# Second network: other places in memory for the activation tiles, and one load ahead of another

## The chip, the cores and the metric

The kernel runs on one core of one Trainium2 chip. The metric is the device time of one launch in microseconds (us). The engines are TensorE (PE, with its weight loads as PEld), VectorE (DVE), ScalarE (ACT), GpSimd (POOL) and SyncE (SP); SP issues nearly all transfers between HBM and the on-chip memory in this part of the program.

## The reference

The reference chains three stages: a thresholded attention, a layer of eight experts (each token goes to one), and a dense two-layer network. The last one, cut to what matters here:

```python
def _moe2_ref(x, w_in, w_out, alpha) -> np.ndarray:      # x (2304, 512), w_in (512, 2048), w_out (2048, 512)
    h = x @ w_in
    g = np.maximum(h, 0.0) + alpha * np.minimum(h, 0.0)
    return (g @ w_out).astype(np.float32)
```

Here x is the output of the expert layer; its gate weight is multiplied onto the result of the dense network, at the end.

## The kernel before

All matrix products are done in split form: each fp32 operand is cast to a high part and a low part (fp32r), and three products (high by high, high by low, low by high) are summed. So every operand costs a cast on ACT and a subtraction on DVE or POOL before PE can use it.

**The expert layer** (`experts`) runs over 8 experts by 8 chunks of 128 hidden columns, 64 steps of the index g. PE computes `l` (lines 1059 to 1061) and then `y` (1096 to 1098). After the last chunk of an expert its result is copied from PSUM to the tile `yT` (line 1104, ACT and DVE share the work for the last expert) and written to HBM as `yt_d` (line 1114).

**The second network** (`network`) takes its tokens from `yt_d`, in three rounds of 768 tokens, each in two halves of 384. A half is loaded (line 1474) and split into `yh` and `yl` (lines 1481 and 1482). Per round there are 16 chunks of 128 hidden columns times 2 halves, so 32 steps; a step is one hidden block. `f1` computes a block: 12 matmuls into one of two PSUM banks `h` (lines 1552 to 1554), then DVE makes `t` out of it in two instructions (1556 and 1557; the second frees the bank), ACT casts it to `gh` (1559) and POOL subtracts to `gl` (1560). Two steps later `f2mm` multiplies that block with a chunk of `w_out`: 9 matmuls, in threes of which two read `gh` and one reads `gl` (1570 to 1572). So PE's order is f1 of block one, f1 of block two, f1 of block three, f2mm of block one, f1 of block four, f2mm of block two, and so on.

**The weights of the second network** come as 64-bit numbers and are converted chunk by chunk (`conv`): 16 chunks of `w_in` and the first of `w_out` during the expert layer, the other 15 of `w_out` during the first round. A chunk is loaded by `cvload` (line 1423 for `w_out`) into one of two buffers `raw`. ACT takes its absolute value (1436), DVE makes `f` (1438, 1440, 1442), ACT casts it into the weight tile (1447), DVE makes `r` (1449, 1450; the last read of the buffer), and POOL finishes (1452, 1453). The tokens of a half go into the same two `raw` buffers, except those of the very first half, which use the tile `xs` of the expert layer. `y2["limit"]` is the number of chunks that may have been asked for; `cvload` does nothing beyond it.

**What sets the order.** The scheduler is off (`manual_schedule`): each engine runs its instructions as the code is written. The turn of g = 59 issues the load of the first half (`first`), that of g = 60 issues the second (`second`). Semaphore waits are made by the framework, from the tiles: a tile that is laid over the place of an older one waits for everything that still reads or writes the older one.

**Where the tiles lie.** Pools are laid out one behind another, in the order in which they are opened, and those of the second network begin where those of the experts began. In bytes per partition from that start, the experts' tiles are: `stg` 2080 to 18464, `xs` 18464 to 26656, the weight rings `w1` and `w2` 26656 to 59424, the tokens `x` 59424 to 82464, `h` 82464 to 89376, `yT` 89376 to 96288. Over these lie, before: `os` and the second half's `yh`, `yl` 0 to 20480, the `w_out` chunks 1 to 15 20480 to 81920, `gh` 81920 to 88064, `gl` 88064 to 94208, `t` 94208 to 97280.

Of the kernel before, what the change touches and what calls it, by code (L numbers as in the profile page):

```python
# [28 lines left out]
KF2 = FF2 // 128  # L29
# [123 lines left out]
def attn_moe_ffn(ctx: ExitStack, tc, q, k, v, tau, emb, mtau, w1, w2, w_in, w_out, alpha, out):  # L153
# [1244 lines left out]
    def shared(st, general):  # L1398

        y2 = {}  # L1400
# [4 lines left out]
        y2["wo"] = WO  # L1405
        WO[0] = cv_p.tile([128, 2, DM], F32R, tag="wo0", name="wo0", bufs=1)

        y2["limit"] = KF2 + (1 if general else 2)

        def rawtile():  # L1410
            return cv_p.tile([128, 4 * HB], U32, tag="raw", name="raw")
# [59 lines left out]
        def load(q, hf, t):  # L1471
            y2["yg", hf] = t = t.rearrange("p (k n) -> p k n", k=KD)
            n0 = q * NB + hf * HB
            nc.sync.dma_start(t, yt_d[:, :, n0:n0 + HB])
# [12 lines left out]

        def second(p):
            load(0, 1, rawtile().bitcast(F32))

        y2["load"], y2["split"] = load, split
        y2["ahead"] = [first, second] + [lambda p, c=c: [split(0, x) for x in c] for c in ((), (0,), (1, 2, 3))]
# [2 lines left out]
    def network(general, y2):  # L1495
# [3 lines left out]
        def npool(name, **kw):  # L1499
            return f2.enter_context(tc.tile_pool(name=name, reuse_waits="tile", **kw))  # L1500

        os_p = npool("os", bufs=4)
        if general:
            y2["pool", 0] = npool("yT2", bufs=1)
        y2["pool", 1] = npool("yT3", bufs=1)
        wo_p = npool("wo", bufs=1)
        WO = y2["wo"]
        for c in range(1, KF2):
            WO[c] = wo_p.tile([128, 2, DM], F32R, name=f"wo{c}")
        g_p = npool("g", bufs=4)  # L1510
        t_p = npool("tt", bufs=2)
        ps_h = npool("ps_h", bufs=2, space=PSUM)
        ps_o = npool("ps_o", bufs=2 * HT, space=PSUM)
        G = {}
# [121 lines left out]
    with tc.If(far == 0) as near:  # L1636
        with ExitStack() as st:
            y2 = shared(st, False)
            experts(CAPS_NEAR, False, y2)
            network(False, y2)  # L1640
    with near.Else():
        with ExitStack() as st:
            y2 = shared(st, True)
            experts(CAPS_FAR, True, y2)
            network(True, y2)
# [27 lines left out]
```

## Time and profile before

| what | us |
|---|---|
| median of 3 runs (lowest 1065.16, highest 1066.11) | 1065.36 |
| the profiled execution, its own time | 1063.56 |
| its span, first to last instruction | 1061.4 |

The mean granted TensorE clock of that execution was 0.982 of full speed. Busy times: PE 1008.0 us (95% of the span), DVE 708.5 (67%), POOL 529.0 (50%), ACT 507.6 (48%). The expert layer ends and the second network begins at about 640 us. A timeline row reads: start in us, duration in us, engine, line, operation, output<-input, shapes, count; in square brackets the time that the engine was idle before it and what ended that.

### The profile page before, as it was taken

The page shows a single profiled execution, that of the slowest core. Times are in us where ns is not written, and L with a number is a line of the kernel's source. Part 1 is how long each engine was busy: PE and PEld are TensorE (multiplying, and loading weights), DVE is VectorE, ACT ScalarE, POOL GpSimd, SP SyncE. Part 2 cuts the span into 40 slices and gives each one's busy share as a digit, 9 for nine tenths or more (in the row PEclk, how much of TensorE's full clock was granted, in tenths as well). Part 3 has the DMA queues.
Part 4 walks back from the last instruction along what each step waited for, and adds up shares of the span by engine and source line. Part 5 has one row for each costly group of instructions (what it writes and reads, how often), then busy time and mean ns, then how long its engine had stood idle before and what let it go on. Part 6 is the DMA issues. An engine that isn't in the chain of part 4 may idle for free. (4 is left out here: it accounts for less than half of the span.)

```text
span 1061.4 us, 17732 instructions
## 1 busy us (share of the span) xinstructions
PE 1008.0 (95%) x6224; PEld 908.6 (86%) x6224; DVE 708.5 (67%) x1501; ACT 507.6 (48%) x1074; POOL 529.0 (50%) x610
## 2 busy tenths in 40 slices
PE   7999999999999849999999997999999999999995
PEld 6888888878888738999999996999999999999995
DVE  8988888898889747787868887889642222422321
ACT  5777777788777534555546553232231111311112
POOL 6688786888886432222355223756533222332223
PEclk9999999999999979999999998999999999999998
DMA  4265564433321066686988854222220000000001
GB/s 117 66 186 164 155 170 139 120 116 89 80 67 40 1 200 226 191 266 180 242 204 195 246 166 111 80 63 77 80 90 30 1 1 1 31 30 1 1 1 63
DMA packets 100098, 113.67 MB, mean 107 GB/s; under 512 B 22072, under 2 KB 81464, under 8 KB 100000
## 3 DMA queue, kind: packets, MB, share of 16 engines
q1 hardware_dynamic: 96544, 102.99, 34.5%
q0 software_dynamic: 3456, 9.46, 2.4%
q8 instruction: 51, 0.84, 0.3%
q14 instruction: 47, 0.39, 0.1%
HBM read 75.21 MB, written 28.36 MB: 98 GB/s over the span
## 5 line engine op out<-in xcount | busy, mean ns | idle before, releaser
L1560 POOL TENSOR_TENSOR gl<-t,gh 128x384 fp32r<-128x384 f32 x96 | 102.5, 1068 | 246.5 <-ACT gh L1559 246.5
L1556 DVE TENSOR_SCALAR t<-h,alpha_t 128x384 f32<-128x384 f32 x96 | 59.1, 616 | 206.2 <-PE h L1554 200.7
L1559 ACT CAST gh<-t 128x384 fp32r<-128x384 f32 x96 | 49.3, 513 | 271.3 <-DVE t L1557 162.8
L530 DVE TENSOR_REDUCE mx<-s 128x1 f32<-128x576 f32 x144 | 108.1, 754 | 25.5 <-PE s L523 24.1
L546 DVE SCALAR_TENSOR_TENSOR p<-s,mx,e 128x576 f32<-128x576 f32 x144 | 115.9, 810 | 10.8 <-ACT e L539 7.8
L539 ACT ACTIVATE e<-s,mx 128x576 f32<-128x576 f32 x144 | 107.2, 746 | 14.9 <-DVE mx L530 13.6
L1004 DVE TENSOR_TENSOR w<-stg,w 128x512 fp32r<-128x512 f32 x128 | 107.8, 858 | 9.1 <-ACT w L1003 8.5
L1572 PE MATMUL o<-wo,gl 128*128 128x512 f32 x288 | 113.3, 394 | 0.0
L1571 PE MATMUL o<-wo,gh 128*128 128x512 f32 x288 | 113.1, 393 | 0.0
L1570 PE MATMUL o<-wo,gh 128*128 128x512 f32 x288 | 112.3, 390 | 0.0
L559 PE MATMUL t<-ident,p 128*128 128x128 f32 (+1 forms) x720 | 107.6, 277 | 3.6 <-DVE ptl L377 1.1
L559 PEld LDWEIGHTS t<-ident,p 128*128 128x128 f32 (+1 forms) x720 | 80.9, 137 | 7.5 <-ACT pt L586 3.4
L523 PE MATMUL s<-ks,qs 128*128 128x288 f32 x256 | 80.6, 330 | 6.2 <-DVE p L546 5.3
L1003 ACT CAST w<-stg 128x512 fp32r<-128x512 f32 x128 | 76.7, 619 | 15.8 <-DMA stg<-in_moe_w_dram 15.8
L1097 PE MATMUL y<-h,w 128*128 128x256 f32 (+6 forms) x256 | 80.2, 313 | 2.8 <-DVE h L1065 2.8
L1096 PE MATMUL y<-h,w 128*128 128x256 f32 (+6 forms) x256 | 82.3, 321 | 0.0
L1060 PE MATMUL l<-x,w 128*128 128x256 f32 (+6 forms) x256 | 79.8, 312 | 0.3 <-DVE x L1048 0.2
L1059 PE MATMUL l<-x,w 128*128 128x256 f32 (+6 forms) x256 | 79.9, 312 | 0.0
L1098 PE MATMUL y<-h,w 128*128 128x256 f32 (+6 forms) x256 | 79.6, 311 | 0.0
L1061 PE MATMUL l<-x,w 128*128 128x256 f32 (+6 forms) x256 | 79.5, 310 | 0.0
L523 PE MATMUL s<-kx,qs 128*128 128x288 f32 x256 | 72.9, 299 | 0.2
L1554 PE MATMUL h<-yh,wi_b 128*128 128x384 f32 x216 | 73.0, 338 | 0.0
(233 smaller groups left out, 2756.1 us busy)
## 6 DMA issues: line engine op xcount, KB each, us to landing
stg<-in_moe_w_dram SPq DMA_DIRECT2D x64, 512.0 KB, 5.4
kx<-ks SPq DMA_DIRECT2D x60, 144.0 KB, 2.5
xd<-zt SPq DMA_DIRECT2D x8, 1024.0 KB, 7.5
raw<-in_moe_w_in_dram SPq DMA_DIRECT2D x16, 512.0 KB, 3.7
raw<-in_moe_w_out_dram SPq DMA_DIRECT2D x16, 512.0 KB, 3.5
rawk<-in_k_dram SPq DMA_DIRECT2D x16, 256.0 KB, 2.9
rawq<-in_q_dram SPq DMA_DIRECT2D x16, 256.0 KB, 2.9
yd<-zt SPq DMA_DIRECT2D x4, 1024.0 KB, 6.8
```

The costliest lines, as they stand in the source:

```text
L523: nc.tensor.matmul(s[:, hf, 0:288], lt, st[nm, a][:, hf * 288:(hf + 1) * 288], start=(j == 0 and x == 0), stop=(j == n - 1 and x == 1))
L530: nc.vector.tensor_reduce(out=mx[:, 0:1], in_=st["s", t][:, :, 0:288], op=ALU.min, axis=AX.XY)
L539: nc.scalar.activation(e, st["s", t][:, :, 0:288], AF.Exp, bias=st["mx", t][:, 0:1], scale=-1.0)
L546: nc.vector.scalar_tensor_tensor(out=p.rearrange("q (a b) -> q a b", a=2), in0=st["s", t][:, :, 0:288], scalar=st["mx", t][:, 2:3], in1=st ...
L559: nc.tensor.transpose(m[0:w, j * n + i * 128:j * n + (i + 1) * 128], st["p", t][:, c * 128:c * 128 + w], ident)
L1004: nc.vector.tensor_tensor(t[:, 1], src, t[:, 0].bitcast(F32), op=ALU.subtract)
L1096: nc.tensor.matmul(m[:, 0:n], w[:, 0, dsl], h[:, 0, 0:n], start=(f == 0), stop=False)
L1097: nc.tensor.matmul(m[:, 0:n], w[:, 0, dsl], h[:, 1, 0:n], start=False, stop=False)
L1560: nc.gpsimd.tensor_tensor(gl, g, gh.bitcast(F32), op=ALU.subtract)
L1570: nc.tensor.matmul(m, gh[:, ts], WO[f][:, 0, :], start=(f == 0), stop=False)
L1571: nc.tensor.matmul(m, gh[:, ts], WO[f][:, 1, :], start=False, stop=False)
L1572: nc.tensor.matmul(m, gl[:, ts], WO[f][:, 0, :], start=False, stop=(f == KF2 - 1))
```

## The change

Two edits. The pools of `gh`/`gl` and of `t` are opened ahead of the pool of the `w_out` chunks. And the limit on chunks is one lower until `second` has taken its buffer; `second` then raises it by one. On the path that these inputs take, `general` is false.

```diff
-        y2["limit"] = KF2 + (1 if general else 2)
+        y2["limit"] = KF2 + 1
...
         def second(p):
             load(0, 1, rawtile().bitcast(F32))
+            y2["limit"] += 1
...
         y2["pool", 1] = npool("yT3", bufs=1)
+        g_p = npool("g", bufs=4)
+        t_p = npool("tt", bufs=2)
         wo_p = npool("wo", bufs=1)
         WO = y2["wo"]
         for c in range(1, KF2):
             WO[c] = wo_p.tile([128, 2, DM], F32R, name=f"wo{c}")
-        g_p = npool("g", bufs=4)
-        t_p = npool("tt", bufs=2)
```

With it the second network's tiles lie, from the same start: `gh` 20480 to 26624, `gl` 26624 to 32768, `t` 32768 to 35840, the `w_out` chunks 1 to 15 35840 to 97280, of which chunk 14 is at 89088 to 93184 and chunk 15 at 93184 to 97280. From line 1490 on, a line of the changed kernel has a number one higher than its counterpart before (`t` is made at 1557 and 1558, `gh` at 1560, `gl` at 1561).

SP's queue at the end of the expert layer. `xs<-yt_d` and `raw<-yt_d` are the tokens of the first and the second half, `raw<-in_moe_w_out_dram` are chunks of `w_out`, `yt_d<-yT` is the last expert's result; names such as DMAHW7 are the semaphores of single transfers. Before:

```order
L1474 DMA xs<-yt_d 128x4x384 [waits DMAHW5_49,DMAHW4_49,PE_49]
L1486 DMA gs<-pd 128x18x2 [waits DMASW3_49]
L1423 DMA raw<-in_moe_w_out_dram 128x1024 [waits DMAHW7_49,DVE_49,Activation_49]
L1474 DMA raw<-yt_d 128x4x384 [waits DMAHW0_49,DMAHW2_49,DVE_49,Activation_49]
L1114 DMA yt_d<-yT 512x1x288 [waits DMAHW1_49,DMAHW0_49,DMAHW5_49,DVE_49,Activation_49]
L1423 DMA raw<-in_moe_w_out_dram 128x1024 [waits DVE_49]
```

And now:

```order
L1474 DMA xs<-yt_d 128x4x384 [waits DMAHW5_49,DMAHW4_49,PE_49]
L1486 DMA gs<-pd 128x18x2 [waits DMASW3_49]
L1474 DMA raw<-yt_d 128x4x384 [waits DMAHW7_49,DVE_49,Activation_49]
L1423 DMA raw<-in_moe_w_out_dram 128x1024 [waits DMAHW0_49,DMAHW2_49,DVE_49,Activation_49]
L1114 DMA yt_d<-yT 512x1x288 [waits DMAHW5_49,DMAHW1_49,DMAHW7_49,DVE_49,Activation_49]
L1423 DMA raw<-in_moe_w_out_dram 128x1024 [waits DVE_49]
```

The second half's tokens and the second `w_out` chunk have changed places, and with them the two `raw` buffers and their waits: the tokens now wait for the last `w_in` chunk's buffer, the chunk for the first `w_out` chunk's.

DVE at the same place: the last copies of `yT`, the second half's subtractions (`yl<-raw,yh`), then the first hidden block's `t`. Before:

```order
L1104 COPY yT<-y_8654 128x288 [waits DMAHW4_49,PE_49]
L1104 COPY yT<-y_8662 128x288 [waits PE_49]
L1482 TENSOR_TENSOR yl_8978<-raw,yh_8977 128x384 [waits DMAHW0_49,DVE_49,Activation_49]
L1482 TENSOR_TENSOR yl_8978<-raw,yh_8977 128x384 [waits Activation_49] x3
L1556 TENSOR_SCALAR t<-h,alpha_t 128x384 [waits DMAHW1_49,DVE_49,PE_49]
L1557 SCALAR_TENSOR_TENSOR t<-h,t 128x384 [waits DVE_49]
```

And now:

```order
L1104 COPY yT<-y_8654 128x288 [waits DMAHW4_49,PE_49]
L1104 COPY yT<-y_8662 128x288 [waits PE_49]
L1482 TENSOR_TENSOR yl_8978<-raw,yh_8977 128x384 [waits DMAHW7_49,DVE_49,Activation_49]
L1482 TENSOR_TENSOR yl_8978<-raw,yh_8977 128x384 [waits Activation_49] x3
L1557 TENSOR_SCALAR t<-h,alpha_t 128x384 [waits PE_49]
L1558 SCALAR_TENSOR_TENSOR t<-h,t 128x384 [waits DVE_49]
```

The order on DVE is unchanged. The first `t` waited for a transfer (DMAHW1) besides PE and now waits for PE alone.

POOL around the first `gl`, with the end of the first `w_out` chunk ahead of it and the second chunk behind. Before:

```order
L1453 TENSOR_TENSOR wo_5804<-f,r 128x512 [waits DVE_49,Pool_49]
L1560 TENSOR_TENSOR gl<-t,gh 128x384 [waits DMAHW3_49,DMAHW2_49,DMAHW4_49,DMAHW1_49,DMAHW5_49,DMAHW0_49,DMAHW6_49,PE_49,Activation_49]
L1560 TENSOR_TENSOR gl<-t,gh 128x384 [waits Activation_49]
L1452 TENSOR_TENSOR f<-f,wo_8950 128x512 [waits DVE_49]
L1453 TENSOR_TENSOR wo_8950<-f,r 128x512 [waits DMAHW5_49,DMAHW6_49,DMAHW3_49,DMAHW7_49,DVE_49,Pool_49]
```

And now:

```order
L1453 TENSOR_TENSOR wo_5804<-f,r 128x512 [waits DVE_49,Pool_49]
L1561 TENSOR_TENSOR gl<-t,gh 128x384 [waits DMAHW3_49,DMAHW4_49,DMAHW2_49,DMAHW5_49,DMAHW1_49,DMAHW6_49,DMAHW0_49,DMAHW7_49,PE_49,Activation_49]
L1561 TENSOR_TENSOR gl<-t,gh 128x384 [waits PE_49,Activation_49]
L1452 TENSOR_TENSOR f<-f,wo_8956 128x512 [waits DVE_49]
L1453 TENSOR_TENSOR wo_8956<-f,r 128x512 [waits DVE_49,Pool_49]
```

The order on POOL is unchanged too. The first `gl` waits for transfers in both, the rows do not tell which transfer of each semaphore; the first chunk of `w_out` that is converted in this stage no longer does.

## Rows read from the trace of the kernel before

**Rows 1.** Windows: us, then busy us per engine, granted clock, DMA share, GB/s.

```profile
640.00:656.00 16.00, 9.41 (x44) 8.51 (x44) 8.81 (x18) 4.41 (x10) 1.01 (x1) 0.79 0.48 112
656.00:850.00 194.00, 194.00 (x976) 176.04 (x975) 119.89 (x173) 47.81 (x90) 98.34 (x83) 1.00 0.19 60
850.00:1046.00 196.00, 196.00 (x988) 178.11 (x987) 60.02 (x102) 30.81 (x62) 53.48 (x53) 1.00 0.02 9
```

**Rows 2.** Waits, 630 to 700 us: who waited for whom, total, times, longest.

```profile
PE h L1552 <- DVE t L1557: 5.9, 1, 5.9
DVE t L1556 <- DMA yt_d<-yT: 5.5, 1, 5.5
...
ACT yh L1481 <- DMA raw<-yt_d: 2.0, 1, 2.0
```

**Rows 3.** Timeline of PE.

```profile
642.65 0.34 PE L1554 MATMUL h<-yh,wi 128*128 128x384 f32 x1
...
652.23 0.69 PE L1552 MATMUL h<-yh,wi 128*128 128x384 f32 x1 [5.89 <-DVE t L1557]
...
655.92 0.40 PE L1570 MATMUL o<-wo,gh 128*128 128x512 f32 x1
...
658.03 0.34 PE L1552 MATMUL h<-yh,wi 128*128 128x384 f32 x1
...
660.15 0.39 PE L1570 MATMUL o<-wo,gh 128*128 128x512 f32 x1
```

**Rows 4.** Windows of 2 us within the transition, columns as in rows 1.

```profile
646.00:648.00 2.00, 0.34 (x2) 0.01 (x1) 0.00 (x0) 0.00 (x0) 0.00 (x0) 1.00 0.88 142
...
650.00:652.00 2.00, 0.00 (x0) 0.00 (x0) 1.00 (x2) 0.00 (x0) 0.00 (x0) 0.50 0.21 12
```

**Rows 5.** Timeline of SP.

```profile
631.12 0.63 SPq L1474 DMA_DIRECT2D xs<-yt_d  x1
...
632.53 3.38 SPq L1423 DMA_DIRECT2D raw<-in_moe_w_out_dram  x1
637.27 0.58 SPq L1474 DMA_DIRECT2D raw<-yt_d  x1
643.15 0.63 SPq L1114 DMA_DIRECT2D yt_d<-yT  x1
```

**Rows 6.** Transfers issued from 615 to 690 us: KB each, median us to landing.

```profile
xs<-yt_d SPq DMA_DIRECT2D x1, 768.0 KB, 5.1
...
yt_d<-yT SPq DMA_DIRECT2D x1, 576.0 KB, 7.7
```

**Rows 7.** Line 1423, all 16 loads of `w_out` chunks.

```profile
DMA to landing us min/median/max: 3.4/3.5/6.6
```

**Rows 8.** Timeline of ACT.

```profile
640.55 0.40 ACT L1104 COPY yT<-y 128x288 f32<-128x288 f32 x1 [0.39 <-PE y L1098]
642.97 1.76 ACT L1481 CAST yh<-raw 128x384 fp32r<-128x384 f32 x4 [2.02 <-DMA raw<-yt_d]
644.63 0.67 ACT L1436 ACTIVATE f<-raw 128x512 f32<-128x512 f32 x1
```

**Rows 9.** Timeline of DVE.

```profile
641.18 0.81 DVE L1104 COPY yT<-y 128x288 f32<-128x288 f32 x2
643.52 1.96 DVE L1482 TENSOR_TENSOR yl<-raw,yh 128x384 fp32r<-128x384 f32 x4 [1.53 <-ACT yh L1481]
650.97 0.62 DVE L1556 TENSOR_SCALAR t<-h,alpha_t 128x384 f32<-128x384 f32 x1 [5.49 <-DMA yt_d<-yT]
651.62 0.56 DVE L1557 SCALAR_TENSOR_TENSOR t<-h,t 128x384 f32<-128x384 f32 x1
...
654.97 0.56 DVE L1557 SCALAR_TENSOR_TENSOR t<-h,t 128x384 f32<-128x384 f32 x1
...
657.62 1.39 DVE L1438 TENSOR_SCALAR f<-f 128x512 f32<-128x512 f32 x1
```

**Rows 10.** Timeline of POOL.

```profile
652.86 1.01 POOL L1560 TENSOR_TENSOR gl<-t,gh 128x384 fp32r<-128x384 f32 x1 [12.95 <-ACT gh L1559]
```

## The prediction

> **What bounds the kernel now.** I read the windows first, to see where PE, the busiest engine, is not busy. From 656 to 1046 us it is busy for every one of the 390 us at the full clock, so in that stretch nothing but PE's own work counts, and whatever moves PE's arrival at 656 us moves the end by as much [rows 1]. In the 16 us ahead of it PE is busy for only 9.41 us, at a mean granted clock of 0.79 [rows 1]. That is the hand-over from the expert layer to the second network, and the change touches it.
>
> The waits tell why [rows 2]: PE waits 5.9 us, once, for DVE's `t`, and DVE waits 5.5 us, once, for the transfer `yt_d<-yT`. The reader is to see one chain. The last expert's result is issued at 643.15 [rows 5] and lands 7.7 us later [rows 6]. Only then, at 650.97, does DVE begin the first `t` [rows 9]. It is done at 651.62 + 0.56 = 652.18, which frees the PSUM bank, and PE starts its third hidden block at 652.23 [rows 3]. The numbers in `t` have nothing to do with that transfer. What ties them is the place: `t` lies at bytes 94208 to 97280, over `yT` at 89376 to 96288, which the transfer still reads. While PE stands idle its clock falls from 1.00 to 0.50 of full speed, that is from 2.4 to 1.2 GHz [rows 4], so the third block, 12 matmuls, takes 655.92 - 652.23 = 3.69 us; the fourth takes 660.15 - 658.03 = 2.12 [rows 3].
>
> A smaller wait comes ahead of it. ACT idles 2.0 us for the second half's tokens, `raw<-yt_d`, and starts to split them at 642.97 [rows 2, 8]. They were issued only at 637.27, behind the second `w_out` chunk [rows 5].
>
> **The change part by part.** It adds and removes no instruction; it moves tiles, and exchanges two loads.
>
> *The place of `t`, `gh`, `gl`.* Now `t` and `gl` lie over the ring `w1` and `gh` over `xs`. The last readers are PE's `l` matmuls, ACT's and DVE's splitting of the first half, all over before DVE's copies of `yT` end at 641.18 + 0.81 = 641.99 [rows 9]. So the first `t` waits for PE and for its turn on DVE alone, as DVE's order shows. Over `yT` come the `w_out` chunks 14 and 15, which the code converts in the last turns of the first round, some 28 steps later; the transfer is over by then, and I cost that at nothing. Were it not over, POOL would wait there and PE's `f2mm` of chunk 14 behind it.
>
> *The tokens ahead of the chunk.* They take the place at 632.53 [rows 5]; the buffer is free there, since the chunk could be issued into it. No row shows their landing from this place, so I bound it. Early end: 5.1 us after issue, as the first half's tokens of the same size took [rows 6], 637.6. Late end: the chunk in this place took at most 6.6 us for 512 KB [rows 7], by size 6.6 x 768/512 = 9.9 us, 642.4. I take 640.5, an estimate nearer to the late end, because `xs<-yt_d` is under way until 631.12 + 5.1 = 636.2 and the two share the engines. What decides is whether they are there when ACT has copied its share of `yT`, at 640.55 + 0.40 = 640.95 [rows 8]. With 640.5 they are.
>
> One might fear that the bigger load slows `xs<-yt_d`, which ACT needs at once. In the trace the chunk was issued 1.41 us behind it [rows 5], and it still landed 5.1 us after its own issue [rows 6]. The Trainium skill (DMA: Bandwidth & Descriptors, Queues, rings and completion order) says that transfers of one issuing engine share a row of rings, that a DMA engine takes descriptors in ring order, and that completion is nevertheless not in order. By the first half of the rule the sum stands as below; by the second `xs` could lose time to the 256 KB more behind it, a third of its own size, and the sum would be smaller by about a third of 5.1 us, 1.7.
>
> *The sum*, in the order of the engines.
> ACT starts the second half's casts at 641.0 instead of 642.97. DVE follows as soon as it is free: its four subtractions take 1.96 us [rows 9], 641.99 + 1.96 = 643.95. The two `t` instructions take 652.18 - 650.97 = 1.21 us [rows 9], so the bank is free at 645.16, and with the hand-over of 0.05 (652.23 - 652.18) PE may start the third block at 645.2.
> PE itself: the first block's last matmul starts at 642.65 [rows 3], and 0.17 us later (2.12/12) the second block follows without the gap for tokens, until 642.82 + 2.12 = 644.94. It then waits 0.3 us for the bank, far too short for the clock to fall as it did (it was still at 1.00 in the first 2 us of the idle time [rows 4]). The third block ends at 645.2 + 2.12 = 647.3.
> Then `f2mm` of block one. The first `gl` was ready at 652.86 + 1.01 = 653.87, 1.69 us behind `t` [rows 9, 10]; now 645.16 + 1.69 = 646.85, in time. It starts at 647.3 instead of 655.92 [rows 3]: 8.6 us earlier, of which 652.23 - 645.2 = 7.0 are waiting and 3.69 - 2.12 = 1.6 clock.
>
> Does PE keep it? DVE gains only 652.18 - 645.16 = 7.0, so its lead over PE shrinks by 1.6. The fourth block started at 658.03 [rows 3], its bank had been free since 654.97 + 0.56 = 655.53 [rows 9]: a lead of 2.5 us, now 0.9. It holds. After that the third `w_out` chunk is the late one: its load is issued when the tokens' buffer is free, 643.95, and lands at most 6.6 us later [rows 7], at 650.55; with ACT's 0.67 [rows 8] DVE can begin it at 651.2, while the order would want it at 657.62 - 7.0 = 650.6 [rows 9]. 0.6 us late, inside the lead. The second chunk, issued at 637.27 now, must be there when ACT has cast the tokens, at 641.0 + 1.76 = 642.8; by the 6.6 it lands at 643.9 at the latest, and the first `gh`, behind it on ACT, is due at 645.2 (643.9 + 0.67 = 644.6). Hidden.
>
> Bounds of the sum: if PE never waits it is 655.92 - (644.94 + 2.12) = 8.9. If the tokens land at 642.4, DVE's subtractions begin 0.55 us later (643.52 - 642.97), `t` is done at 642.95 + 1.96 + 1.21 = 646.1, the third block starts at 646.2, and the gain is 7.6.
>
> Span 1061.4 - 8.6 = 1052.8; the profiled execution 1063.56 - 8.6 = 1055.0. The median of the runs was 1.8 above the profiled execution, so 1065.36 - 8.6 = 1056.8 is the time I predict.
>
> **The rivals.**
> *The first `gl` still waits for `yT`.* POOL's row still names transfers, DMAHW1 among them, and that is the semaphore on which `t` waited. If it means the last result, issued at about 642.1 now, `gl` begins at 642.1 + 7.7 = 649.8 and is ready at 650.9, while PE has its third matmul of `f2mm` at 647.8 (nine of them take 658.03 - 655.92 = 2.11, so the third comes 0.5 after the first). PE loses 3.1 us and, as the pause is as long as the one that cost the clock, up to 1.6 more: a gain of about 4.7 to 3.9, 1061.1. Against it: `gl` at 26624 to 32768 shares no byte with `yT`; its first 32 bytes lie over `xs`, which ends at 26656 and was filled by many older transfers, and that explains the list.
> *DVE becomes the bound.* The lead of 0.9 is thin, and DVE's instructions are uneven: 1.39 us for a line that POOL's work beside it stretches [rows 9]. Each such stretch beyond the lead costs about 1.39 - 0.9 = 0.5; with the late third chunk, two to four of them, 1 to 2 us: 1058.3. By the Trainium skill (SBUF — State Buffer, Who interferes with whom) whichever of DVE and GpSimd comes first keeps the shared port for its whole instruction, so a DVE instruction can lose a whole POOL instruction's time; that would make each stretch 1.0 (the 1.01 of rows 10) and this rival 1 to 3 us. For it: the lead. Against it: the stall's end leaves the two engines' relative order as it was.
> *Slower: the second chunk blocks ACT.* It now queues behind 768 KB of tokens, and ACT's absolute value of it stands ahead of the first `gh`. If it lands at T, the first `gl` is ready at T + 0.67 + 1.69, and PE, whose clock would have fallen, pays 1.6 as well. Before, the third matmul of `f2mm` came at 655.92 + 0.5 = 656.4. The change becomes a loss from T = 656.4 - 4.0 = 652.4, 15 us after issue; at T = 656 it would be 3.6 slower, 1069. Against it: no chunk took more than 6.6 [rows 7], and the longest transfer of the place 7.7 [rows 6].
> *The change doesn't do what it says*: another old reader holds the new places, and DVE waits as before, 1065.4. DVE's order, where the transfer is gone from the first `t`, speaks against it.
>
> **How the numbers follow.** My forecast has 0.72, with a range of its own of 1056.0 to 1058.0 (the sum's bounds, and half a us for the spread of the runs). DVE as the bound, or tokens at the late end and more, 0.11; `gl` waiting, 0.06; more than the sum, through a wait that I don't see, 0.04; no effect 0.04; slower 0.03. A measurement of this kernel can tell 0.2%, 2.1 us, from no change, so faster means under 1063.2: 0.72 + 0.11 + 0.06 + 0.04 = 0.93. Same 0.04, slower 0.03. The range from 1055.2 to 1060.2 takes in the forecast, the DVE rival and part of the rest.
>
> **What would show it.** In the profile after: no wait of DVE's first `t` for a transfer, and PE's wait for `t` at the third block under 1 us (if it is still 3 us or more, the place of `t` was not what held it). `raw<-yt_d` issued at about 632.5, ACT casting from about 641 without idling. A granted clock of 1.00 in all windows from 640 to 656 us, and the first `f2mm` at about 647.3. PE busy without a break from there on; new waits of PE for `t` in the first ten blocks would speak for DVE as the bound, a wait for `gl` for the first rival, ACT idle ahead of line 1436 for the slower one. If the span is shorter by less than 7 us, a step of the sum is wrong.

## The result, and the profile after

The changed kernel takes 1057.22 us in the median of 6 runs (1053.46 to 1057.59); the kernel before, run beside it, 1065.28 (1065.06 to 1066.11). The ratio is 0.9917, with a 95% interval from 0.9903 to 0.9931: 0.0083 of 1065.28 is 8.8 us faster, with the interval 7.4 to 10.3; the two medians alone lie 8.1 us apart. Forecast were 8.6 us and 1056.8 us.

The profiled execution of the changed kernel took 1056.95 us, its span 1055.1. Its times can't be laid over those of before directly: it reached the last `y` matmul of the expert layer 2.36 us later, as one row of the kernel before (timeline of PE) shows against the first row of the fence after it.

```profile
640.62 0.29 PE L1098 MATMUL y<-h,w 128*128 128x288 f32 x1
```

The timeline of PE after the change: the last `y` matmul, the first matmuls of the second network's second and third hidden blocks, of the first `f2mm` and of the fourth block. Lines below the edit have moved by one.

```profile
642.98 0.30 PE L1098 MATMUL y<-h,w 128*128 128x288 f32 x1
...
645.20 0.34 PE L1553 MATMUL h<-yh,wi 128*128 128x384 f32 x1
...
647.40 0.45 PE L1553 MATMUL h<-yh,wi 128*128 128x384 f32 x1
...
649.59 0.39 PE L1571 MATMUL o<-wo,gh 128*128 128x512 f32 x1
...
651.69 0.34 PE L1553 MATMUL h<-yh,wi 128*128 128x384 f32 x1
```

So I count from the last `y` matmul. Before, the third block followed 652.23 - 640.62 = 11.61 us later and the first `f2mm` 15.30 [rows 3]; now it is 647.40 - 642.98 = 4.42 and 6.61. `f2mm` is 8.69 us earlier. The third block, from its first matmul to `f2mm`, takes 2.19 where it took 3.69, and the fourth block starts 8.71 after the last `y` matmul where it was 17.41. PE waits no more, and works at the full clock; the windows (columns as in rows 1) answer to [rows 1, 4]:

```profile
640.00:656.00 16.00, 15.62 (x87) 14.30 (x87) 13.71 (x24) 7.30 (x16) 7.66 (x7) 1.00 0.82 183
...
650.00:652.00 2.00, 2.00 (x10) 1.64 (x10) 1.93 (x5) 0.76 (x2) 0.66 (x1) 1.00 1.04 102
...
656.00:850.00 194.00, 194.00 (x979) 176.44 (x978) 120.84 (x171) 47.30 (x88) 95.74 (x82) 1.00 0.18 58
```

The reader is to see 15.62 of 16 us busy at a granted 1.00, for 9.41 at 0.79. The waits of 630 to 700 us answer to [rows 2]; the 5.9 us of PE and the 5.5 of DVE are gone, and the longest wait for a transfer is a new one, of ACT for a `w_out` chunk:

```profile
ACT f L1436 <- DMA raw<-in_moe_w_out_dram: 3.0, 1, 3.0
DVE f L1438 <- ACT f L1436: 2.0, 1, 2.0
...
ACT yh L1481 <- DMA xs<-yt_d: 0.6, 1, 0.6
...
PE y L1097 <- DVE h L1065: 0.4, 1, 0.4
...
ACT yh L1481 <- DMA raw<-yt_d: 0.3, 1, 0.3
```

The timeline of SP shows the exchanged loads, and `yT`'s issue between the second and the third chunk; it answers to [rows 5]:

```profile
633.76 0.63 SPq L1474 DMA_DIRECT2D xs<-yt_d  x1
...
635.18 3.80 SPq L1474 DMA_DIRECT2D raw<-yt_d  x1
639.64 0.36 SPq L1423 DMA_DIRECT2D raw<-in_moe_w_out_dram  x1
644.50 0.63 SPq L1114 DMA_DIRECT2D yt_d<-yT  x1
646.25 5.92 SPq L1423 DMA_DIRECT2D raw<-in_moe_w_out_dram  x2
```

The transfers' rows (KB each, us from issue to landing), one from each of three stretches, answer to [rows 6, 7]; the last is the third chunk:

```profile
xs<-yt_d SPq DMA_DIRECT2D x1, 768.0 KB, 5.6
...
yt_d<-yT SPq DMA_DIRECT2D x1, 576.0 KB, 9.2
...
raw<-in_moe_w_out_dram SPq DMA_DIRECT2D x1, 512.0 KB, 7.9
```

And the timelines of ACT, DVE and POOL, put together in order of time; they answer to [rows 8 to 10]:

```profile
643.61 1.76 ACT L1481 CAST yh<-raw 128x384 fp32r<-128x384 f32 x4 [0.29 <-DMA raw<-yt_d]
...
646.15 0.60 DVE L1557 TENSOR_SCALAR t<-h,alpha_t 128x384 f32<-128x384 f32 x1
...
646.79 0.56 DVE L1558 SCALAR_TENSOR_TENSOR t<-h,t 128x384 f32<-128x384 f32 x1
...
648.03 1.02 POOL L1561 TENSOR_TENSOR gl<-t,gh 128x384 fp32r<-128x384 f32 x1 [5.76 <-ACT gh L1560]
...
650.16 0.56 DVE L1558 SCALAR_TENSOR_TENSOR t<-h,t 128x384 f32<-128x384 f32 x1
...
654.25 0.67 ACT L1436 ACTIVATE f<-raw 128x512 f32<-128x512 f32 x1 [2.98 <-DMA raw<-in_moe_w_out_dram]
...
654.95 0.61 DVE L1438 TENSOR_SCALAR f<-f 128x512 f32<-128x512 f32 x1 [2.05 <-ACT f L1436]
```

`yT` is issued at 644.50 and lands at 653.7, and the first `t` starts at 646.15 without a bracket: it no longer waits for that transfer. `t` is done at 647.35 and PE starts at 647.40.

### The profile page after: what moved, and what is told of

It is laid out like the page before. It is cut to its first block, busy times and chain, and to the rows that moved or that the text cites. A ratio compares the mean times of both kernels' runs of the same rounds, so it can differ in the third digit from the quotient of the medians.

```text
span 1055.1 us, 17731 instructions
## 1 busy us (share of the span) xinstructions
PE 1009.3 (96%) x6224; PEld 911.2 (86%) x6224; DVE 710.7 (67%) x1501; ACT 508.0 (48%) x1074; POOL 529.1 (50%) x610
```

## The experiments

All kernels' times are given beside the kernel before on the same chip. There its median was 1069 to 1070 us, not 1065.3. The table has, for one profiled execution of each: the start of the last `y` matmul; from there to the third block; from the third block to the fourth; from there to the span's end; then the timed ratio.

| kernel | last `y` | to third | to fourth | rest | ratio, 95% |
|---|---|---|---|---|---|
| before, first trace | 640.62 | 11.61 | 5.80 | 403.4 | |
| before again (`c_before`) | 640.56 | 12.80 | 7.11 | 403.3 | 1.0003 [0.9986, 1.0021] |
| after | 642.98 | 4.42 | 4.29 | 403.4 | 0.9917 [0.9903, 0.9931] |
| after again (`c_after`) | 644.37 | 4.41 | 4.32 | 403.4 | 0.9905 [0.9882, 0.9928] |
| `e1_places` | 642.47 | 6.19 | 4.28 | 403.6 | 0.9902 [0.9883, 0.9921] |
| `e2_order` | 646.65 | 11.41 | 6.70 | 403.8 | 0.9980 [0.9963, 0.9997] |
| `e3_gl_over_yT` | 645.15 | 4.42 | 11.16 | 404.8 | 0.9958 [0.9943, 0.9973] |
| `e4_yT_elsewhere` | 642.12 | 6.45 | 4.29 | 403.3 | 0.9909 [0.9887, 0.9931] |
| `e5_keep_clock` | 644.62 | 13.71 | 5.83 | 403.4 | 0.9987 [0.9966, 1.0009] |
| `e6_one_load_less` | 641.92 | 4.43 | 4.29 | 403.4 | 0.9892 [0.9868, 0.9916] |
| `e7_elsewhere_and_order` | 645.51 | 4.41 | 4.29 | 403.4 | 0.9915 [0.9889, 0.9941] |
| `e8_keep_clock_longer` | 648.09 | 13.66 | 4.20 | 403.4 | 0.9984 [0.9967, 1.0001] |

Two things come before any verdict. The rest is the same 403.3 to 403.6 us in ten of the twelve, so the columns between hold nearly the whole effect. And the arrival at the last `y` matmul moves by 7.5 us between executions without regard to the edit: `e8` and `e5` share all their work ahead of it with the kernel before, and arrive at 648.09 and 644.62 where that arrives at 640.62 and 640.56. A difference of two spans carries this scatter; the columns between don't.

### The two kernels again

> The kernel before once more, as a control of what the other runs are compared with: a ratio of 1 to itself within its interval, and from the last y matmul of the expert layer to the first f2mm 15.3 us, as in the first trace. If the timed ratio or the hand-over differ from that, the larger gains that the timed runs of the first four experiments showed beside their traces (some 3 us each) come from the comparison and not from the kernels.

> The changed kernel once more, beside the control: hand-over of 6.6 us, so 8.7 us less than before by the traces; the timed ratio near 0.992. If the timed gain is again some 3 us more than the hand-over's, something outside it differs.

Nothing is edited. After behaves as it did (8.73 us from the last `y` matmul to the fourth block, for 8.71), although the third `w_out` chunk lands later still, 9.1 us after its issue, and DVE waits 3.3 us for it (waits of 630 to 700 us):

```profile
DVE f L1438 <- ACT f L1436: 3.3, 1, 3.3
```

Before doesn't: 19.91 us, for 17.41 in the first trace. Its `yT` lands 8.7 us after issue, for 7.7; DVE waits 6.5 us and PE 6.9, and the third block runs all of its 4.0 us at half the clock. The timelines of DVE and of PE:

```profile
652.10 0.62 DVE L1556 TENSOR_SCALAR t<-h,alpha_t 128x384 f32<-128x384 f32 x1 [6.51 <-DMA yt_d<-yT]
```

```profile
640.56 0.29 PE L1098 MATMUL y<-h,w 128*128 128x288 f32 x1
...
653.36 0.69 PE L1552 MATMUL h<-yh,wi 128*128 128x384 f32 x1 [6.94 <-DVE t L1557]
...
657.37 0.63 PE L1570 MATMUL o<-wo,gh 128*128 128x512 f32 x1
...
660.47 0.34 PE L1552 MATMUL h<-yh,wi 128*128 128x384 f32 x1
```

`f2mm`'s first matmul too takes 0.63 us, where it took 0.40 [rows 3]. So what there was to gain is 17.4 - 8.7 = 8.7 us by one execution and 19.9 - 8.7 = 11.2 by the other; the timed gain here is 10.2 us (7.7 to 12.6). The experiments below are held against this second trace, as their chips show the same longer time of before. That is a choice, as this execution, of 1066.04 us, is the shortest of its twelve; by the first trace each gain below that is counted to the fourth block is 2.5 us smaller.

### The places alone

```
+        g_p = npool("g", bufs=4)
+        t_p = npool("tt", bufs=2)
         wo_p = npool("wo", bufs=1)
         ...
-        g_p = npool("g", bufs=4)
-        t_p = npool("tt", bufs=2)
```

> The kernel before with the first edit alone: the pools of gh/gl and t ahead of the w_out chunks; tokens and second chunk in the old order. Theory (the place of t made PE wait for the last result's transfer): the tokens still come at about 643, DVE's subtractions end at 645.5, t is done at 646.7, PE's third block starts about 0.5 us after the second has ended instead of 5.9 us; the clock stays at 1.00. First f2mm 5.5 + 1.6 = 7.1 us earlier, 1058.2 us. Rival (the order of the two loads is what counts, because the last result can only be written when the tokens have been read): at most 3 us faster, 1062 or more.

The wait for `yT` goes, and the clock stays: 10.47 us to the fourth block, 9.4 less than before again; timed 10.5 us less (8.4 to 12.5). The 7.1 us expected were worked out from the first trace, and by that it is 17.41 - 10.47 = 6.9. The timelines of DVE, whose first `t` waits for nothing now, and of PE:

```profile
647.40 0.61 DVE L1556 TENSOR_SCALAR t<-h,alpha_t 128x384 f32<-128x384 f32 x1
```

```profile
645.54 0.45 PE L1552 MATMUL h<-yh,wi 128*128 128x384 f32 x1 [0.69 <-ACT yh L1481]
...
648.66 0.44 PE L1552 MATMUL h<-yh,wi 128*128 128x384 f32 x1 [0.34 <-DVE t L1557]
...
650.85 0.40 PE L1570 MATMUL o<-wo,gh 128*128 128x512 f32 x1
...
652.94 0.34 PE L1552 MATMUL h<-yh,wi 128*128 128x384 f32 x1
```

What is left is ACT, whose late tokens cost PE 0.69 ahead of the second block: 10.47 to 8.71 is 1.76 us, the part of the other edit by the traces. The timed ratios of `e1` and after overlap and can't tell 1.8 us.

### The order of the loads alone

```
-        y2["limit"] = KF2 + (1 if general else 2)
+        y2["limit"] = KF2 + 1
         ...
         def second(p):
             load(0, 1, rawtile().bitcast(F32))
+            y2["limit"] += 1
```

> The kernel before with the second edit alone: the second half's tokens ahead of the second w_out chunk; all tiles in their old places. Theory: the first t still waits for the last result's transfer, which is issued about 1 us earlier because it need not wait for the tokens' landing; PE's wait stays above 5 us and so does the fall of the clock; about 1.0 us faster, 1064.3 us. Rival (the order counts): 5 us or more faster, 1060 or less.

18.11 us to the fourth block, 1.8 less than before again, and 0.5 of it lost in the rest; timed 2.1 us less (0.3 to 4.0). `yT` is issued 1.50 us after the last `y` matmul starts (648.15), for 2.53 and 2.70 in the two traces of before, but lands 8.6 us later, and DVE and PE wait as long as ever (timelines of DVE, of PE):

```profile
656.79 0.62 DVE L1557 TENSOR_SCALAR t<-h,alpha_t 128x384 f32<-128x384 f32 x1 [6.91 <-DMA yt_d<-yT]
```

```profile
658.06 0.69 PE L1553 MATMUL h<-yh,wi 128*128 128x384 f32 x1 [6.95 <-DVE t L1558]
```

So the edit alone removes ACT's short wait for the tokens, and not the long one for `yT`. It issues the transfer that is waited for 1.0 to 1.2 us sooner, and that is inside the timed interval; the rest of the 1.8 is no more than what the two traces of before differ by (2.5).

### `yT` moved away, all else left

```
+        yt_p = mpool("yt", bufs=1)
         xt_p = mpool("xt", bufs=1)
         ...
-        yt_p = mpool("yt", bufs=1)
```

> The kernel before with the experts' pool of yT opened ahead of that of the tokens x: all tiles of the second network stay in their old places, but yT lies at 59424 to 66336, under w_out chunks 10 to 12, and t and gl lie over h. Theory (the overlap of t with yT is the cause, whatever way it is undone): the same 7.1 us as the first edit alone, 1058.2 us, and no wait of DVE for the transfer. Rival (the gain of the change comes from the w_out chunks' new places, since the first converted chunk no longer waits for transfers): no change, 1065.3 us.

This undoes the same overlap from its other side: `t`, `gh`, `gl` and the chunks keep their old places. 10.74 us to the fourth block, 9.2 less than before again, 6.7 by the first trace; timed 9.7 us less (7.4 to 12.1). With `e1` it shows that the overlap of `t` with `yT` was the cause, not a good of the new places. The timelines of DVE and of PE:

```profile
647.32 0.61 DVE L1556 TENSOR_SCALAR t<-h,alpha_t 128x384 f32<-128x384 f32 x1
...
648.57 0.45 PE L1552 MATMUL h<-yh,wi 128*128 128x384 f32 x1 [0.32 <-DVE t L1557]
```

DVE's `t` no longer waits for the transfer, and PE waits 0.32 us for `t`, as it does in `e1` (0.34).

### `yT` moved away, and the order

The edits of `e4` and `e2` together.

> yT moved as in the fourth experiment, and the tokens ahead of the second chunk; the second network's tiles in their old places. Theory (two causes that add: the overlap of t with yT, and, once it is gone, the tokens' lateness): from the last y matmul to the fourth hidden block 8.7 us as in the changed kernel, where the fourth experiment alone had 10.7 and before 17.4 to 19.9; timed like the changed kernel, a ratio near 0.991. Rival (the tokens' order helps only with the new places): 10.7 us, as the fourth experiment.

8.70 us to the fourth block: the same as after, to 0.01 us, with other places. By the traces the order brings 10.74 - 8.70 = 2.04 us here and 1.76 beside the new places. Timed it is 9.1 us less (6.3 to 11.9), which overlaps `e4`'s interval: the 2 us of the order are shown by the traces alone.

### Only `t` moved, `gh` and `gl` left on `yT`

```
-        g_p = npool("g", bufs=4)
         t_p = npool("tt", bufs=2)
         wo_p = npool("wo", bufs=1)
         ...
+        g_p = npool("g", bufs=4)
```

(against after; `gl` then lies at 91136 to 97280)

> The changed kernel with the pool of gh/gl opened behind the w_out chunks: t lies at 20480 to 23552 over xs, but gl at 91136 to 97280 lies over yT. Theory: the first t does not wait, PE runs its third block at once, but the first gl waits for the transfer until about 8.3 us behind its issue, PE stands about 3 us at the third matmul of the first f2mm and loses up to 1.6 us by its clock: 3.8 to 5.4 us faster than before, 1060 to 1061.5 us. Rival (only the place of t counts, the lead of gl hides its wait): as the changed kernel, 8 us or more faster, 1057.2 us.

The third block is as early as in after (4.42 us), and then PE stands for 5.2 us in the middle of the first `f2mm`, and its clock falls (0.50 in the windows from 658 to 662 us): 11.16 us from the third block to the fourth, and 1.4 us more than usual in the rest. From the last `y` matmul to the end that is 2.9 us less than before again; timed 4.5 us less (2.9 to 6.1). In the timelines of ACT and PE, and in the waits:

```profile
656.42 0.51 ACT L1560 CAST gh<-t 128x384 fp32r<-128x384 f32 x1 [4.67 <-DMA yt_d<-yT]
```

```profile
657.58 0.80 PE L1573 MATMUL o<-wo,gl 128*128 128x512 f32 x1 [5.19 <-POOL gl L1561]
```

```profile
POOL gl L1561 <- DMA raw<-in_moe_w_out_dram: 12.1, 1, 12.1
```

`yT` was issued at 646.66, so it landed after some 9.7 us. The last row is one to distrust: the wait of POOL is put down to a `w_out` load, but it ends when ACT's wait for `yT` ends. So the first rival's mechanism is real; in after it is not there, as `gl` has no byte in common with `yT` and POOL starts when ACT's `gh` is done.

### The clock alone: useless matmuls in the pause

```
+            if s == 2 and not general:
+                idle = ps_o.tile([128, 512], F32, tag="o", name="o")
+                wi0 = WI(0).rearrange("p x (k j) -> p x k j", k=KD)
+                for _ in range(30):
+                    nc.tensor.matmul(idle[:, 0:HB], wi0[:, 0, 0, :], y2["y", 0][0][:, 0, :], start=True, stop=True)
```

(against before; 46 in the second version)

> The kernel before with 30 matmuls of no use (128x384, into a PSUM bank that is overwritten later) issued on PE ahead of the third hidden block, so that PE is busy while it waits for t. Theory (8.6 us are 7.0 of waiting and 1.6 of clock): t still waits for the transfer, the third block starts at the same time, but at the full clock it takes 2.1 us instead of 3.7: 1.6 us faster, about 1063.7 us where before takes 1065.3. Rival (the slow clock hides under other waits and costs nothing): no change.

> The kernel before with 46 instead of 30 matmuls of no use ahead of the third hidden block, so that PE is busy until t is done. Theory: the clock stays at 1.00, and from the start of the third block to the start of the fourth PE takes 4.3 us as in the changed kernel, where before took 5.8 in one execution and 7.1 in another: 1.5 to 2.8 us faster than before, a ratio of 0.997 to 0.9985. Rival (something besides the clock slows the third block, such as the late transfer): 5.8 us or more in spite of a busy PE.

Thirty were too few: they end at 655.96, PE idles 2.37 us, and the clock falls all the same, after PE has started again. In the windows of `e5`:

```profile
656.00:658.00 2.00, 0.00 (x0) 0.00 (x0) 0.90 (x2) 0.00 (x0) 0.00 (x0) 1.00 0.09 8
658.00:660.00 2.00, 1.67 (x9) 1.67 (x10) 1.93 (x4) 0.52 (x1) 1.01 (x1) 0.91 0.00 0
660.00:662.00 2.00, 2.00 (x7) 1.90 (x6) 1.94 (x4) 0.89 (x2) 0.00 (x0) 0.50 0.00 0
```

Forty-six cover the pause. `t` is late (done at 660.04), the matmuls outlast it by 1.7 us, and the blocks then run as in after (timeline of PE in `e8`):

```profile
653.62 8.29 PE L1620 MATMUL o<-yh,wi 128*128 128x384 f32 x46
661.75 0.34 PE L1552 MATMUL h<-yh,wi 128*128 128x384 f32 x1
...
663.86 0.39 PE L1570 MATMUL o<-wo,gh 128*128 128x512 f32 x1
...
665.95 0.34 PE L1552 MATMUL h<-yh,wi 128*128 128x384 f32 x1
```

Third block to fourth: 4.20 us, for 5.80 and 7.11 in the two traces of before, with the same late `t`. That difference, 1.6 to 2.9 us, is clock alone. In the timed runs it can't be told from nothing: the matmuls themselves came too late by as much, and both intervals hold 1.

### One `w_out` load less ahead of the first round

```
-        for _ in range(2 if general else 1):
+        for _ in range(2 if general else 0):
             cvload()
```

(against after)

> The changed kernel without the load of a w_out chunk that is issued ahead of the first round, so that every chunk's load starts only when the chunk before it is converted. Tests how much lead the conversion has: the third chunk comes about 3 us later still and each conversion (about 6 us of DVE with POOL beside it) waits 3.5 us for its load, 9.5 us per chunk where PE takes 8.5. If the lead is as thin as the prediction's DVE rival has it, PE waits for t or for weights, 5 to 10 us in the sum, 1062 to 1067 us; if the lead is larger, as the changed kernel, 1057 us.

The loss didn't come, but this run doesn't test the lead, because the edit moved nothing on the chip. The third chunk's load is issued 645.20 - 641.92 = 3.28 us after the last `y` matmul, for 646.25 - 642.98 = 3.27 in after, and the fourth's 8.86 us after it in both. The timeline of SP, with the two loads in one row:

```profile
645.20 5.91 SPq L1423 DMA_DIRECT2D raw<-in_moe_w_out_dram  x2
```

In the code the call stands later now. But SP has nothing else to issue between the old place and the new one, so each load keeps its place in SP's queue and the buffer that it waits for. What I expected, loads that start only when the chunk ahead is converted, was a misreading of the code. So `e6` is the changed kernel a third time: 8.72 us to the fourth block, a ratio of 0.9892 (interval overlapping after's).

What the traces do show of the lead is a chunk that was late by itself: in `c_after` DVE lost 3.3 us to the third chunk, and PE did not wait from the last `y` matmul to the end of its work. How much later a chunk would have to come to reach PE was not tried. No kernel tried is shown to beat after; in after's hand-over only some 0.1 us of waiting is left.

## Why the prediction was right

*What held PE.* Right, and shown from two sides: `e1` and `e4` take the overlap of `t` with `yT` away in different places and both lose the 5 to 7 us of waiting; `e2`, which keeps the overlap, keeps the wait.

*The size.* `f2mm` was to come 8.6 us earlier, with bounds of 7.6 and 8.9; it came 8.69 earlier. PE was to reach the third block at 645.2, 4.6 us behind the last `y` matmul; it was 4.4. The share of the clock was put at 1.6 us; the third block gave back 3.69 - 2.19 = 1.5, and `e8` gives 1.6 from the third block to the fourth on the first trace's terms. That the timed gain met the sum this closely owes something to the execution that I had: in the other trace of before the same hand-over cost 2.5 us more, 1.2 of waiting and 1.3 of clock, and a sum from that would have been 11.2, against a timed 8.8 on the first chip. The first trace's `yT` landed after 7.7 us, the shortest of the nine traces that show this landing.

*The tokens.* Estimated to land 8.0 us after issue; ACT started on them 8.4 us after it (643.61 - 635.18), having idled 0.3. The fear that `xs` loses time to the bigger load was put at up to 1.7 us; `xs` took 5.6 us for 5.1, ACT waited 0.6 for it, and nothing of it reached PE. Nor is the 0.5 shown to come from the order: `xs` took 5.1 to 5.6 us in five traces with the tokens behind it and 5.1 to 5.4 in five with the chunk. The Trainium skill (DMA: Bandwidth & Descriptors, Queues, rings and completion order) has descriptors taken in ring order, and yet completion not in order; these traces bear out the first half of the rule more nearly than the second.

*The lead at the fourth block.* Forecast 0.9; the bank was free at 650.16 + 0.56 = 650.72 and the block started at 651.69, 0.97. It held.

*The third chunk.* Wrong in size. "lands at most 6.6 us later" took the longest of sixteen landings for a bound; in the new surroundings it took 7.9, with `yT`'s 576 KB issued 1.75 us ahead of it. DVE lost 2.0 us there, not 0.6. It stayed hidden: PE waited for nothing behind the hand-over, here or in `c_after`, where the chunk took 9.1 us and DVE lost 3.3.

*The rivals.* The waiting `gl` was not there in after, but its price was wrong: 3.1 us of waiting by a landing of 7.7, and up to 1.6 of clock. In `e3` PE stood 5.2 us, because `yT` took 9.7. On the first trace's terms that kernel would have gained 0.4 us over before, where I had put 3.9 to 4.7 (and where the same terms, 8.6 less 3.1 and less up to 1.6, give 3.9 to 5.5). That DVE becomes the bound, that the second chunk blocks ACT (it landed in time: ACT took it up at 645.27 with no wait), and that nothing changes: none of these came.

*The criterion.* The sentence "If the span is shorter by less than 7 us, a step of the sum is wrong" was itself wrong. The span is 6.3 us shorter and each step of the sum stands. The other 2.4 us went ahead of the change's place. Two windows there, of before and then of after, show a lower granted clock and almost the same work:

```profile
0.00:40.00 40.00, 31.87 (x204) 28.08 (x205) 34.64 (x101) 25.02 (x52) 23.37 (x60) 0.91 0.38 92
...
370.00:410.00 40.00, 24.88 (x122) 19.12 (x121) 20.56 (x60) 17.84 (x40) 10.43 (x10) 0.83 0.66 217
```

```profile
0.00:40.00 40.00, 31.87 (x190) 28.52 (x191) 33.20 (x97) 23.29 (x48) 22.19 (x57) 0.83 0.39 92
...
370.00:410.00 40.00, 25.40 (x112) 19.84 (x111) 18.71 (x60) 16.18 (x38) 8.87 (x9) 0.66 0.65 216
```

Before is at 0.91 and 0.83, after at 0.83 and 0.66. What sets the clock in these two stretches from one execution to the next wasn't tried and stays open; that the arrival scatters in kernels that are the same up to there is in the table above.

## What to carry to other kernels

An engine that waits for a transfer out of a tile whose numbers it doesn't need is waiting for the tile's place: look at what lies on those bytes, and move either of the two. Count such a gain from a mark just ahead of the change to one just behind it, in more than one execution of the kernel before, since spans also carry what happened earlier. Before a landing time from one row is used as a price or a bound, look for the same transfer in other executions. And before a run is read as the answer to a question, look in its trace whether the edit moved what it was to move.

## What was not expected of the hardware

- The same transfer of 576 KB out of `yT` took from 7.7 to 10.1 us from issue to landing in nine traces; one row of one execution is a poor bound.
- Behind a pause of 2.37 us the granted clock fell to 0.50, and it fell only after PE had been at work again (`e5`). For the same code behind a pause of 5.9 and of 6.9 us, the two blocks' turn took 5.80 and 7.11 us.
- A 512 KB load that lands in 3.6 us in the median of its line took 7.9 us in after and 9.1 in `c_after`, behind `yT`'s transfer.
